# RWKV-6 attention woven into an MLP mixer: the loads of r and k as pieces of their own, the halves of y around the next unit's state products and gram, new sequences

## Chip, core and metric

The kernel runs on one core of one Trainium2 chip. The metric is the device time of one execution in microseconds (us). Five engines run side by side: PE (TensorE, matmul), DVE (VectorE), ACT (ScalarE), POOL (GpSimd) and SP (SyncE, which issues nearly all transfers). Each works through its own instructions in program order and waits for the others by semaphores.

## The reference

Attention in four batches, eight heads of 48, 768 steps; its output is laid out as (batch, 768, 384) and goes through a mixer over tokens (768 to 256 to 768) and one over channels (384 to 1536 to 384).

```python
for t in range(S):
    cur = einsum('bhd,bhe->bhde', u[None] * k[t], v[t])
    y[t] = einsum('bhd,bhde->bhe', r[t], state + cur)
    state = w[t][..., None] * state + einsum('bhd,bhe->bhde', k[t], v[t])
x = y.transpose(0, 2, 1, 3).reshape(B, S, H * D)

h = maximum(x.transpose(0, 2, 1) @ w_tok1, 0) @ w_tok2
u = x + h.transpose(0, 2, 1)
out = u + maximum(u @ w_ch1, 0) @ w_ch2
```

All of it is float32.

## The kernel before

**Units.** The 768 steps of a batch are cut into three units of 256 steps (two chunks of 128 rows); there are twelve, 0 to 11, and units 3b to 3b + 2 are batch b. For a unit DVE builds products of the decays w by two scans (`ends`, L435, and `begins`, L443), multiplies k by the one (`keys`, L440) and r by the other (`queries`, L446). PE transposes the keys (`tokens`, L345, into k_ps), ACT copies them out (`copied0`, `copied1`, L350), and PE forms k times v for the state (`carry`, L365, the state products, into kv_ps). ACT and DVE take turns at carrying the state over four steps (`by0` to `by3`, L501, and `up0` to `up3`, L514 and L516). `gram` (L315) is r times k within 64 steps, masked by DVE (`mask`, L488), which releases its two banks. `sums0` to `sums2` and `put` (L463 to L473) put in the diagonal.

**The two halves of y.** `before` (L380) multiplies r by the states that stood before each block, into two banks of y_ps; ACT reads one column of each (`seen`, L392), and `after` (L401) adds the part from within the blocks, with vt and at. ACT copies y to x in three pieces (`taken0` to `taken2`, L407); `taken0` releases the first bank, `taken1` and `taken2` the second. `tokens`, `carry`, `gram`, `before` and `after` are each made of many small products, 8 transposes or 64 matmuls of 64 by 48 or 64 elements.

**Dependencies between units.** `keys` of a unit needs the loads that the unit before it started; `by1` of a unit needs `before` of the unit before, `mask` needs its `after`, and the load of v is issued behind `after` and `carry`.

**The mixer** of a batch: `hidden` (L662) forms the first token sums from the six chunks of x, two chunks for each unit; `back` (L693, L702) the second; `turn` (L708) transposes, with forms by ACT (L710) and DVE (L711), joined at L634. The channel part takes two half batches of 384 columns, each in two halves of six sums. An up sum is nine products of 128x384: three at L739, three at L741 with a weight tile from the ring, three at L746. ACT (L721, L724), DVE (L728) and POOL (L732) make the three forms of it (`high`, `scaled`, `z`). `down` (L757 to L759) multiplies these by the second weights, three products for each sum and each 128 columns; DVE adds the result to x (L765), SP stores it (L767). A ring of ten tiles holds the third forms of the weights; each use of a tile is followed by the load of another (L625, `load_third`), which waits on SP until that use is done. Batch 0's mixer is made of other lines (back L903, turn L914, up L934 and L938, down L949, the sum L953).

**PSUM.** kv_ps has banks of its own. All else takes turns in six banks (`bank`): y two, gram two, the transposed keys two, each wide sum one.

**Order.** Batch 0's attention runs in a prologue in an order written out by hand (to about 48 us). After it the mixer of batch bt is woven with the attention of batch bt + 1 by a string `WEAVES[bt]`: `interleaved` takes the next piece of the stream that each digit names. Stream 0 is the mixer (from batch 1 on it has a second for joins, from batch 2 on more for its token weights' forms); the units have one stream each, as the function `attention_pieces` lists them; in batches 0 and 1 a last stream forms weights. The string sets the order on PE, DVE, ACT and SP at once; every engine works its own instructions in that order. Each unit's stream begins with `loads`, which is `load_rk(i + 1)`: four transfers of 192 KB on SP (L168), the halves of k first. Since a unit's pieces stand in one stream, their order among themselves is fixed by the function, `loads` ahead of all others.

How PE's pieces of a unit (number behind the name) stand among the mixer's pieces (the plain numbers count those), from the three strings; braces hold what follows without a piece of the mixer between:

```
batch 0: 19 {tokens3 own3} 7 {carry3 gram3} 11 {before3} 2 {after3} 13 {tokens4} 6 {carry4 gram4} 12 {before4} 4
         {tokens5} 3 {carry5 after4 gram5} 7 {before5} 1 {after5} 1
batch 1: 12 {tokens6} 3 {carry6 gram6} 19 {before6} 11 {tokens7} 9 {after6 carry7 gram7} 18 {before7} 11
         {tokens8} 5 {carry8 gram8 after7} 13 {before8} 2 {after8} 13
batch 2: 12 {tokens9} 7 {carry9} 7 {gram9} 21 {before9} 5 {tokens10} 8 {carry10 gram10 after9} 17 {before10} 9
         {tokens11} 2 {after10 carry11 gram11} 19 {before11} 2 {after11} 13
```

(`own` is a gram of a batch's first unit with u times k.)

Of the kernel before, what the change touches and what calls it, by code (L numbers as in the profile page):

```python
# [47 lines left out]
LEAST, MOST = 2.0 ** -40, 2.0 ** 40  # L48
MID = 3 * G // 4 * SEG1
WEAVES = [  # L50
    "44140440440000440401041114001004140004404040411441110104414014401041041014144110144140104404110140444000414141004140414"
    "442044444104440214401040404000424420404012404240024022400042242242420242244422044040204442200422044422000202443003334030"
    "43040303443332342344343300343243434334034343243304404300344342403333",
    "050000022220000505250502225052502205522502012100010252000000220200002000200002200200020002000220300000300200330033003030"
    "033000000000030000023330330302000033303033003330000000101103000003300040020400000000204300000040044000444000404443304444"
    "4044040000000440404000400000044003040004040000300444000000000000",
    "204240000022033204220000433322344240400000044440010001100404440000000000044000004040040000400044004000400400404055550000"
    "050505000500000000055000450055450005055055540550500045005050500001101050505606000000000006000400000660606666065606060000"
    "066005066050606660000606000605600000606000600006060660006000000000000000",
    "200202020202023002300320320003300000000011100000000000000000000000000000000000000000000000000000000000000000000000000000"  # L60
    "00001101000000000000000000000000000000000000000000000000000000000000000000000000000000000",
]


# [1 line left out]
def rwkv6_then_mixer(  # L66
# [950 lines left out]
    def interleaved(order, *streams):  # L1017

        left_of = [iter(stream) for stream in streams]
        out = [next(left_of[int(n)])[1] for n in order]  # L1020
        assert not any(True for stream in left_of for _ in stream)
        return out
# [116 lines left out]

    units = {i: unit(i) for i in range(UB, NU)}  # L1140
    attention = {bt: [attention_pieces(i) for i in range(bt * UB, (bt + 1) * UB)] for bt in range(1, B)}

    for bt in range(B):
        if bt == 0:
            early_forms, late_forms = weights_in_turn()
            pieces = interleaved(WEAVES[0], first_mixing(), *attention[1], early_forms)
        elif bt < B - 1:
            pieces = interleaved(WEAVES[bt], *exact_mixing(bt), *attention[bt + 1], *([late_forms] if bt == 1 else []))
        else:
            pieces = interleaved(WEAVES[bt], *exact_mixing(bt))  # L1150
# [134 lines left out]
```

## Time and profile before

| | us |
|---|---|
| median of three runs | 481.99 |
| the three runs | 480.54, 481.99, 482.96 |
| the profiled execution | 482.32 |
| its span in the profile | 480.5 |

The profile is of one execution. A row of the timeline has its start in us, the time from the start of its first instruction to the end of its last, the engine, the line of the kernel, the operation, what it writes and reads, and how many instructions stand in it; in brackets, the time that the engine stood idle before it and what released it. The ends of matmuls are modelled, so durations of neighbours overlap; their starts are what to count with. A row of waits has the engine and the line that waited, the releaser, the total, the number and the longest. A row of the windows has the stretch, then the busy time and the instructions of PE, PE's weight loads, DVE, ACT and POOL, then the granted clock of PE, the share of the transfer engines and their GB/s. A row of a tile has the line, the operation, the count, the shortest, median and longest duration in ns, and its first and last start.

### The profile page before, as it was taken

The page shows a single profiled execution, that of the slowest core. Times are in us where ns is not written, and L with a number is a line of the kernel's source. Part 1 is how long each engine was busy: PE and PEld are TensorE (multiplying, and loading weights), DVE is VectorE, ACT ScalarE, POOL GpSimd, SP SyncE. Part 2 cuts the span into 40 slices and gives each one's busy share as a digit, 9 for nine tenths or more (in the row PEclk, how much of TensorE's full clock was granted, in tenths as well). Part 3 has the DMA queues.
Part 4 walks back from the last instruction along what each step waited for, and adds up shares of the span by engine and source line. Part 5 has one row for each costly group of instructions (what it writes and reads, how often), then busy time and mean ns, then how long its engine had stood idle before and what let it go on. Part 6 is the DMA issues. An engine that isn't in the chain of part 4 may idle for free.

```text
span 480.5 us, 12671 instructions
## 1 busy us (share of the span) xinstructions
PE 464.9 (97%) x5298; PEld 408.3 (85%) x5298; DVE 336.4 (70%) x478; ACT 254.0 (53%) x588; POOL 59.2 (12%) x58
## 2 busy tenths in 40 slices
PE   2999999999999999999999999999999999999995
PEld 2786688866697668999999969999999979999995
DVE  7999899798788778757856298767856365235331
ACT  6689866763779666354546245365536244034040
POOL 1000000000000001230504002140413003032030
PEclk9999999999999999999999999999999999999999
DMA  8956937760684656764847553395605532436221
GB/s 302 330 166 205 280 130 232 260 218 33 179 245 138 194 170 213 218 217 155 229 132 246 205 163 128 116 267 184 191 26 175 193 103 83 121 94 206 87 86 56
DMA packets 49408, 83.77 MB, mean 174 GB/s; under 512 B 4864, under 2 KB 40576, under 8 KB 49344
## 3 DMA queue, kind: packets, MB, share of 16 engines
q1 hardware_dynamic: 49056, 82.80, 54.5%
q8 instruction: 43, 0.70, 0.6%
q14 instruction: 21, 0.17, 0.1%
q10 hardware_dynamic: 288, 0.10, 0.1%
HBM read 71.87 MB, written 11.01 MB: 172 GB/s over the span
## 4 chain that ended last, share of the span: by engine, by line
PE 95%; ACT 2%; DMA 1%; issue 0%; SPq 0%; DVE 0%; DVEq 0%; ACTq 0%
PE h_ps L949 10%; PE ends_ps L739 8%; PE ends_ps L746 8%; PE ends_ps L741 8%; PE o_ps L757 8%; PE o_ps L759 8%; PE o_ps L758 8%; PE z_ps L938 7%; PE h_ps L662 5%; PE gram L315 4%; PE z_ps L934 3%; PE h_ps L693 3%; PE y_ps L380 3%; PE y_ps L401 3%; PE kv_ps L365 2%; PE k_ps L345 2%
## 5 line engine op out<-in xcount | busy, mean ns | idle before, releaser
L732 POOL TENSOR_TENSOR z_high<-z_high 128x384 fp32r<-128x384 f32 x48 | 58.0, 1211 | 404.8 <-DMA ring<-third 188.2
L765 DVE SCALAR_TENSOR_TENSOR x<-o_ps,x 128x384 f32<-128x384 f32 x35 | 19.1, 556 | 54.9 <-PE o_ps L759 54.9
L721 ACT ACTIVATE z_high<-ends_ps 128x384 fp32r<-128x384 f32 x48 | 23.5, 489 | 58.3 <-PE ends_ps L746 58.2
L739 PE MATMUL ends_ps<-x_forms,forms 128*128 128x384 f32 x216 | 50.4, 341 | 0.0
L746 PE MATMUL ends_ps<-z_more,forms 128*128 128x384 f32 x216 | 50.2, 340 | 0.0
L741 PE MATMUL ends_ps<-x_forms,ring 128*128 128x384 f32 x216 | 49.3, 337 | 0.0
L949 PE MATMUL h_ps<-wch,z 128*128 128x384 f32 x144 | 48.6, 490 | 0.0
L728 DVE SCALAR_TENSOR_TENSOR z_high<-ends_ps,z_high 128x384 fp32r<-128x384 f32 x48 | 26.6, 553 | 31.0 <-ACT z_high L721 30.6
L757 PE MATMUL o_ps<-forms,z_high 128*128 128x384 f32 x140 | 47.9, 342 | 0.0
L759 PE MATMUL o_ps<-forms,z_high 128*128 128x384 f32 x140 | 47.1, 337 | 0.0
L758 PE MATMUL o_ps<-ring,z_high 128*128 128x384 f32 x140 | 47.1, 337 | 0.0
L501 ACT ACTIVATE before<-state,to_end 112x48 f32<-112x48 f32 x132 | 33.2, 323 | 18.2 <-DVE state L516 15.9
L949 PEld LDWEIGHTS h_ps<-wch,z 128*128 128x128 f32 x144 | 26.6, 190 | 16.8
L746 PEld LDWEIGHTS ends_ps<-z_more,forms 128*128 128x128 f32 x216 | 38.9, 188 | 0.3 <-DVE z_more L634 0.2
L739 PEld LDWEIGHTS ends_ps<-x_forms,forms 128*128 128x128 f32 x216 | 38.2, 188 | 0.7
L741 PEld LDWEIGHTS ends_ps<-x_forms,ring 128*128 128x128 f32 x216 | 38.5, 188 | 0.0
L938 PE MATMUL z_ps<-xT,wch 128*128 128x256 f32 x144 | 31.8, 380 | 0.0
L938 PEld LDWEIGHTS z_ps<-xT,wch 128*128 128x128 f32 x144 | 27.1, 190 | 3.8
L724 ACT ACTIVATE z_high<-z_high 128x384 fp32r<-128x384 f32 x48 | 25.2, 526 | 3.3
L757 PEld LDWEIGHTS o_ps<-forms,z_high 128*128 128x128 f32 x140 | 26.3, 188 | 0.2
L758 PEld LDWEIGHTS o_ps<-ring,z_high 128*128 128x128 f32 x140 | 26.3, 188 | 0.0
L759 PEld LDWEIGHTS o_ps<-forms,z_high 128*128 128x128 f32 x140 | 26.3, 188 | 0.0
(198 smaller groups left out, 929.6 us busy)
## 6 DMA issues: line engine op xcount, KB each, us to landing
ring<-third SPq DMA_DIRECT2D x144, 192.0 KB, 3.3
raw<-in_w_ch_dram SPq DMA_DIRECT2D x16, 512.0 KB, 4.9
rk<-in_rk_dram SPq DMA_DIRECT2D x36, 192.0 KB, 5.1
near<-in_near_dram SPq DMA_DIRECT2D x8, 768.0 KB, 4.9
w<-in_w_dram SPq DMA_DIRECT2D x10, 520.5 KB, 3.8
vt<-in_v_dram SPq DMA_DIRECT2D x12, 384.0 KB, 4.2
out_dram<-x SPq DMA_DIRECT2D x17, 192.0 KB, 2.5
third<-forms SPq DMA_DIRECT2D x12, 192.0 KB, 3.5
```

The source lines that it names most:

```text
L501: act.mul(t[:ROWS, a], state[bt, g][:ROWS, a], by_last(c, j)[:, a:a + 1])
L724: act.mul(z_form(jt, 2), z_form(jt, 0).bitcast(f32), 1.0 / BASE)
L728: dve.scalar_tensor_tensor(z_form(jt, 1), a, 0.0, z_form(jt, 0).bitcast(f32), op0=ALU.max, op1=ALU.subtract)
L732: pool.tensor_add(z_form(jt, 2), z_form(jt, 2).bitcast(f32), z_form(jt, 1).bitcast(f32))
L739: pe.matmul(a, up[m], xf[0][:, m], start=m == 0, stop=False)
L741: pe.matmul(a, low[:, m], xf[1][:, m], start=False, stop=False)
L746: pe.matmul(banks["a", jt], joint, xf[2][:, m], start=False, stop=m == 2)
L757: pe.matmul(a, z[0], up, start=first, stop=False, skip_group_check=True)
L758: pe.matmul(a, z[1], held[bt, s, half, 1, jt], start=False, stop=False, skip_group_check=True)
L759: pe.matmul(a, z[2], joint, start=False, stop=last, skip_group_check=True)
L938: pe.matmul(ps, now["wch1"][:, m, ts(jt, 128)], xT[:, m, ts(s, SEG)], start=(m == 0), stop=(m == DM // 128 - 1))
L949: pe.matmul(ps, zs[s][:, jt, ts(n, 128)], now["wch2"][:, jt, :], start=(jt == 0), stop=(jt == NJ - 1))
```

## The change

The first piece (`loads`) of each of the three units of a batch is taken out of the unit's stream, and the three form a stream of their own, so that a string can place them anywhere in their order. The streams behind move by one digit. Four new strings are put in. The prologue, the pieces and what each of them waits for are as before.

```diff
@@ -48,17 +48,17 @@
 WEAVES = [
-    "44140440440000440401041114001004140004404040411441110104414014401041041014144110144140144104404110140444000414141004140414"
...
+    "555500055500550050050010510155550505511055500505000551050550511511045515055511010505550105155150051151555151505510515505"
...
 ]
@@ -1139,6 +1139,8 @@
     units = {i: unit(i) for i in range(UB, NU)}
     attention = {bt: [attention_pieces(i) for i in range(bt * UB, (bt + 1) * UB)] for bt in range(1, B)}
+    for of in attention.values():
+        of.append([pieces.pop(0) for pieces in of])

     for bt in range(B):
         if bt == 0:
```

PE's order by the new strings, written as above:

```
batch 0: 25 {tokens3} 1 {own3} 8 {carry3 gram3} 22 {tokens4} 1 {before3 carry4 gram4 after3} 15 {tokens5} 5
         {before4 carry5 gram5 after4} 7 {before5} 1 {after5} 1
batch 1: 12 {tokens6} 6 {carry6 gram6} 39 {tokens7} 11 {carry7 before6 gram7 after6} 30 {tokens8} 5
         {before7 carry8 gram8 after7} 13 {before8 after8}
batch 2: 12 {tokens9} 12 {carry9 gram9} 30 {tokens10} 8 {before9 carry10 gram10 after9} 28 {tokens11} 6
         {carry11 before10 gram11 after10} 20 {before11} 3 {after11} 3
```

In batch 1 `taken2` of unit 7 stands behind unit 8's three copies. In batch 2 the loads for unit 11 stand behind the first six products of the third up sum of the second half batch; between these and the transposes of unit 11's keys PE has that sum's last three products, three more up sums and two groups of three products of `down`. `taken1` and `taken2` of unit 9 stand behind `taken1` of unit 10. Batch 3 has the mixer alone; its string changes the place of some forms and joins at its beginning.

More of the change, by code (lines that the diff above doesn't have):

```diff
@@ L50 @@
 WEAVES = [
[L51 to L60, printed above, removed]
@@ L61 @@
-    "00001101000000000000000000000000000000000000000000000000000000000000000000000000000000000",
+    "555500055500550050050010510155550505511055500505000551050550511511045515055511010505550105155150051151555151505510515505"
+    "015511515555000155550555502000050000002052525002212250215225155251252124552202500502222252055000025050005102333033350020"
+    "3331555035502235323535323550335400353533530305330355503305322353355",
+    "026000020266002066000062002662202000122526210010660260000002000000000002002000002002000022002220203300000000000000000000"
@@ new lines @@
+    "000003000003000300303322300000000303213221130030203000003300000500300300300003000003303300424000200000000000000003444344"
+    "4040000000400030344530004404444004000400004044344400304004444443",
+    "000000404240427220230220330223324034040400004040000111440400040000004004004400000040000000440004000044455000500000000000"
+    "055400054000500000000005005545450405050055555550004055050010001100550000600000070000000000060000600000666660005060606556"
+    "566606066666000066570060000000000000000000000000000564466006000660560660",
@@ L62 @@
+    "002000000022222230330202330002300000010001100000000000000000000000000000000000000000000000000000000000000000000000000000"
+    "00001010100000000000000000000000000000000000000000000000000000000000000000000000000000000",
 ]
```

## The prediction

> **What bounds the kernel now.** I read the page's totals and slices first, then the waits of the matmul engine, four windows by stage, and last the timeline around single units of attention.
>
> ```profile
> span 480.5 us, 12671 instructions
> PE 464.9 (97%) x5298; PEld 408.3 (85%) x5298; DVE 336.4 (70%) x478; ACT 254.0 (53%) x588; POOL 59.2 (12%) x58
> PE   2999999999999999999999999999999999999995
> PE 95%; ACT 2%; DMA 1%; issue 0%; SPq 0%; DVE 0%; DVEq 0%; ACTq 0%
> ```
> ```profile
> PE gram L315 <- ACT near L331: 8.5, 1, 8.5
> PE kv_ps L508 <- ACT before L501: 1.2, 2, 1.0
> PE h_ps L693 <- ACT z_high L686: 0.2, 1, 0.2
> ```
> ```profile
> 0.00:12.00 12.00, 3.54 (x72) 3.23 (x72) 8.48 (x13) 7.47 (x16) 1.26 (x10) 1.00 0.84 303
> 48.00:60.00 12.00, 12.00 (x47) 7.45 (x46) 10.33 (x15) 10.31 (x16) 0.00 (x0) 1.00 0.95 281
> 276.00:288.00 12.00, 11.75 (x52) 8.25 (x50) 11.47 (x15) 5.96 (x10) 0.00 (x0) 1.00 0.57 166
> 456.00:468.00 12.00, 12.00 (x71) 12.00 (x70) 5.02 (x9) 5.06 (x10) 4.05 (x4) 1.00 0.31 95
> ```
>
> PE is busy for 97% of the span and carries 95% of the chain that ended last. Its waits are one of 8.5 us and two of together 1.2 us, both in the prologue, which the change leaves alone, and one of 0.2 us behind it. The windows show what this means by stage: 3.54 of 12 us at the start, 12.00 of 12 from 48 us on, 11.75 where the one late wait falls, at a granted clock of 1.00. So the time after the prologue is the sum of what PE executes, in whatever order. A new order can change it in two ways only: by what it costs PE to go from one kind of product to another, and by making PE wait where it does not now.
>
> **The change, part by part.** The number of matmuls, copies and transfers is the same. What moves is their place.
>
> **Halves of y in runs.** A half of y is 64 small products. One that stands alone among the mixer's 128x384 products:
>
> ```profile
> 231.04 0.70 PE L746 MATMUL ends_ps<-z_more,forms 128*128 128x384 f32 x3
> 231.68 1.15 PE L380 MATMUL y_ps<-before,rk 48*64 48x48 f32 x64
> 232.75 0.80 PE L739 MATMUL ends_ps<-x_forms,forms 128*128 128x384 f32 x3
> 233.39 0.69 PE L741 MATMUL ends_ps<-x_forms,ring 128*128 128x384 f32 x3
> 233.91 0.70 PE L746 MATMUL ends_ps<-z_more,forms 128*128 128x384 f32 x3
> ```
>
> I count from start to start, since the ends are modelled. Three wide products take 0.52 (233.39 to 233.91), but 0.64 ahead of the half and 0.64 behind it; the half takes 1.07. Alone it costs 1.07 + 0.12 + 0.12 = 1.31 us. A half in a run with the state products and the gram:
>
> ```profile
> 214.56 0.69 PE L746 MATMUL ends_ps<-z_more,forms 128*128 128x384 f32 x3
> 215.18 1.15 PE L401 MATMUL y_ps<-vt,at 64*64 64x48 f32 x64
> 216.14 0.90 PE L365 MATMUL kv_ps<-vt,kT 64*48 64x48 f32 x64
> 216.86 1.13 PE L315 MATMUL gram<-rk 48*64 48x64 f32 x64
> 217.92 0.79 PE L739 MATMUL ends_ps<-x_forms,forms 128*128 128x384 f32 x3
> ```
>
> Followed by small products it takes 0.96 (215.18 to 216.14), and the run's two ends are paid by its neighbours anyhow. Joining a lone half saves 1.31 - 0.96 = 0.35. By the two sequences, seven halves that stand alone now come into such runs: both of unit 3 (with unit 4's state products and gram), the first of units 4, 6, 7, 9 and 10. 7 x 0.35 = **-2.45**; bounds 0 (if the gap is not one of switching) and -2.45.
>
> [...]
>
> **State products and gram of unit 9** stand apart now and together then: one entry and one exit fewer, but their neighbours are partly small transposes. Bounds 0 and -0.35, I take the middle, **-0.2**. Moving unit 3's own-gram one wide piece off the transposed keys I cost at nothing (bounds -0.1 and +0.1, the 0.12 of an edge), because the transposes leave no edge behind:
>
> ```profile
> 116.62 0.93 PE L345 MATMUL k_ps<-ident,rk 112*128 112x112 f32 x8
> 117.39 7.92 PE L949 MATMUL h_ps<-wch,z 128*128 128x384 f32 x24
> ```
>
> **The 0.25 us wait** of PE at 284.53 goes: ACT's form there is issued earlier against PE in the new sequence. Bounds 0 and -0.25, **-0.25**.
>
> ```profile
> 284.53 2.35 PE L693 MATMUL h_ps<-z_more,z_high 128*128 128x384 f32 x12 [0.25 <-ACT z_high L686]
> ```
>
> **Unit 8's halves** become neighbours at the end of batch 1's mixing. Between them ACT must read the first (`seen`), which now lies beside wide products:
>
> ```profile
> 163.14 1.15 PE L380 MATMUL y_ps<-before,rk 48*64 48x48 f32 x64
> 164.36 0.22 ACT L392 COPY seen<-y_ps 128x1 f32<-128x1 f32 x2 [1.13 <-PE y_ps L380]
> 164.60 0.47 ACT L407 COPY x<-y_ps 64x384 f32<-64x384 f32 x1
> 166.79 4.14 PE L662 MATMUL h_ps<-x,wtok 128*128 128x384 f32 x12
> 166.89 1.45 ACT L407 COPY x<-y_ps 128x384 f32<-128x384 f32 x3 [0.95 <-PE y_ps L401]
> ```
>
> The second half can start 164.58 - 163.14 = 1.44 after the first. The pair then costs 0.12 + 1.44 + 1.07 + 0.12 = 2.75, against 2 x 1.31 = 2.62 now: **+0.15** (0 if PE's queue hides part of it).
>
> **The first token sums of batch 2** stand right behind. Unit 7's last copy now follows three of unit 8 on ACT; four copies are done 0.10 + 1.45 + 0.47 = 2.0 us after the half ends. The sums of batch 1 took 4.14 for six chunks, 0.69 each, so the third chunk, which needs unit 7, is due at 1.4. **+0.6** (0 to 0.65).
>
> **Loads of r and k.** Each is four transfers on SP's in-order queue; the piece of unit i loads for unit i + 1, so that of unit 11 loads nothing. Seven of the eight others keep ten and more wide sums on PE between them and the transposes that need them, over 15 us. The one for unit 11 comes in batch 2 behind a ring load, which waits for PE's third up sum of that half. Until the transposes of unit 11's keys PE then has 0.52, three sums of nine products and two `down` groups: 0.52 + 3 x 1.57 + 2 x 0.52 = 6.3 us.
>
> ```profile
> SPq L625 <- PE ends_ps L741: 80.8, 57, 13.5
> L168 SPq DMA_DIRECT2D rk<-in_rk_dram x40: 310/420/1327, 1.7 to 313.7; - x40
> L440 DVE TENSOR_TENSOR rk<-rk,to_end x10: 1160/1212/1219, 17.9 to 343.6; 112x1024 f32<-112x1024 f32 x10
> DMA to landing us min/median/max: 3.0/5.2/9.3
> 312.34 1.81 SPq L168 DMA_DIRECT2D rk<-in_rk_dram  x4
> ```
>
> The k halves are issued first: the ring load and two issues at 0.42, a landing, and the keys' product of 1.21: 2.47 + 3.0 = 5.5 us, by the median 7.7, by the longest 11.8. PE would wait 0, 1.4 or 5.5 us. I take **+0.5**, nearer the shortest than the median, since the k halves are the first two of the four that the median counts. The wait holds `keys` on DVE; queued behind it are the `z` of the next up sums, `begins`, `queries` and `up3` of unit 10, so it is paid once, at the transposes or at the `down` products that need `z`. The quartet keeps SP from its ring loads for 1.8 us (312.34); the ring is ten tiles deep, at 0.52 us a tile at the quickest, which covers that; without it 1.8 us at each of the eight, 14 in all.
>
> [...] The trace's shortest landing is 3.0.
>
> `mask` of each next unit also waits for the half that now ends a run. Behind it on DVE are `sums2` and `put`; 7 and more wide pieces stand before the next half, so nothing is added.
>
> **Sum:** -2.45 - 0.2 - 0.25 + 0.15 + 0.6 + 0.5 = -1.65. Against the profiled execution's own 482.32 (its span of 480.5 and 1.8 around it) that is 480.7. It lies 0.33 over the median of the three runs, 481.99, so on the median the forecast is **480.3**. Its own range, with the landing and the joins as unknowns, is 479.0 to 481.8. What a measurement of this kernel can tell from no change is about 0.5%, 2.41 us: the forecast is inside it.
>
> **Rivals.**
> *No new wait.* Joins -2.45, unit 9 -0.35, the wait -0.25, unit 8's pair +0.15: -2.90, **479.1**. For it: the shortest landing. Against: the order of the copies on ACT. Chance 0.16.
>
> *The joins save nothing*, because the gap at an edge is refilled elsewhere: then only -0.25 + 0.15 + 0.6 + 0.5 = +1.0, **483.0**. For it: PE's sums are otherwise gapless, so the edge may be the modelled length of 64 short products. Against: 0.64 and 0.52 are differences of starts. Chance 0.12.
>
> *Unit 11's keys late (slower).* Place: the transposes of unit 11 in batch 2. If the k halves take the longest landing, 9.3, PE waits 5.5 in place of 0.5: -1.65 + 5.0 = +3.3, **485.3**. It decides from a landing of 3.8 (where the wait starts); the whole is no gain from 6.0, and slower than 0.5% from 8.4. For it: ring loads lie in the same queue ahead. Against: the median of 5.2. Chance 0.12.
>
> *Too few banks.* A run holds two y and two gram banks of six at once; in unit 11's, one bank of unit 9's y is still held as well. The next wide sums then wait for releases. With two banks a sum returns its bank after
>
> ```profile
> 231.78 0.49 ACT L721 ACTIVATE z_high<-ends_ps 128x384 fp32r<-128x384 f32 x1 [3.18 <-PE ends_ps L746]
> 232.37 0.56 DVE L728 SCALAR_TENSOR_TENSOR z_high<-ends_ps,z_high 128x384 fp32r<-128x384 f32 x1 [0.32 <-ACT z_high L721]
> 233.01 2.33 DVE L435 TENSOR_TENSOR_SCAN to_end<-w,starts 112x1041 f32<-112x1041 f32 x1
> ```
>
> 232.93 - 231.74 = 1.2 us, and sums come every 1.57, so 2 x 1.57 - 1.57 - 1.2 = 0.4 us are to spare; a scan of 2.33 in between costs 1.9. In two of the seven runs that is 3.8: -1.65 + 3.8, **484.1**. Against: the gram's banks are released before the next scan in the sequences. [...] No row here shows such a wait. Chance 0.08.
>
> That leaves 0.52 for the forecast.
>
> **How the numbers follow.** Faster by over 0.5% is below 479.6: three quarters of the first rival (0.12) and a quarter of the forecast (0.14): 0.26. Slower by over 0.5% is above 484.4: 0.08 of the late keys, 0.04 of the banks, 0.01 of the forecast: 0.13. The rest, 0.61, is no change that can be told. The range reaches 0.7 below the first rival, half of what the quickest of the three runs shown (480.54) lies below their median, and as much above the second (483.0): 478.4 to 483.6. Outside are most of the late keys and banks, some 0.16, and 0.04 below.
>
> **What would show it.** Right: lone halves gone for seven units' halves, with about 0.96 from start to start inside runs of four; PE's waits list with entries of 0.5 or less at the transposes of unit 11 (k_ps, released by the keys' product) and at the token sums of batch 2 (released by copies of y). Wrong: 1.07 and more inside the runs, a wait of PE over 1.5 us for unit 11's keys, or waits of PE for copies and `z` behind the runs. The whole would be wrong if PE's busy time after 48 us rose, since no instruction is added.

## The result and the profile after

The changed kernel takes 486.5 us (median of six runs, 485.99 to 488.13) against 481.74 for the kernel before (480.54 to 482.96, six runs): a ratio of 1.0108, interval 1.0081 to 1.0135. It is 1% slower, outside the range of the prediction. The profiled execution took 486.75, its span is 485.0.

The page of the changed kernel: span and busy times, PE and its granted clock in 40 slices, the row of a transfer queue that brings instructions, and the chain that ended last.

```profile
span 485.0 us, 12673 instructions
PE 462.0 (95%) x5298; PEld 407.0 (84%) x5298; DVE 340.0 (70%) x478; ACT 253.8 (52%) x588; POOL 59.7 (12%) x58
PE   3799999999999999998997999999999999999995
PEclk9889999999999999999998999999999999999998
q8 instruction: 43, 0.70, 0.6%
PE 86%; DMA 5%; ACT 3%; DVE 2%; issue 2%; POOL 1%; SPq 1%; DVEq 0%; ACTq 0%
```

PE executes as many matmuls as before (5298) and is busy for 462.0 us in place of 464.9. Nearly all of this difference lies in the prologue, though: the windows from the first `back` of batch 0 to the end, before and then after, have 425.08 and 424.98 us of PE, in 430.84 and 436.59 us.

```profile
49.66:480.50 430.84, 425.08 (x4303) 376.52 (x4301) 291.82 (x430) 216.86 (x491) 57.98 (x48) 1.00 0.53 165
48.41:485.00 436.59, 424.98 (x4303) 377.88 (x4301) 295.80 (x430) 216.75 (x491) 58.39 (x48) 0.99 0.53 162
```

So PE is busy for as long as before, a stretch at half its clock (below) included; what it has now is holes, in slices 19 and 22 (the dip of the clock in slices 2 and 3 lies in the prologue), and PE's share of the chain falls from 95 to 86%. The waits of PE (total, number, longest):

```profile
PE gram L315 <- ACT near L331: 8.4, 1, 8.4
PE y_ps L401 <- issue: 5.0, 2, 3.6
PE kv_ps L508 <- ACT before L501: 1.2, 2, 1.0
PE k_ps L345 <- PE kv_ps L508: 0.9, 1, 0.9
PE y_ps L401 <- ACT seen L389: 0.6, 1, 0.6
PE kv_ps L365 <- DVE state L516: 0.6, 1, 0.6
PE h_ps L662 <- ACT x L407: 0.4, 1, 0.4
PE y_ps L401 <- ACT seen L392: 0.3, 1, 0.3
PE k_ps L345 <- DVE rk L440: 0.2, 1, 0.2
```

The second row is new and large: two waits, 5.0 us together, in the second half of y, and "issue" means that PE waited for nothing that the profile shows. To place the loss, the spans are cut at rows that both kernels have: the first `back` of batch 0 (L903) and the first token sums of the other batches (L662). Before, then after:

```profile
49.66 1.66 PE L903 MATMUL kv_ps<-h,wtok 128*128 128x384 f32 x4
166.79 8.01 PE L662 MATMUL h_ps<-x,wtok 128*128 128x384 f32 x24
275.25 7.90 PE L662 MATMUL h_ps<-x,x_forms 128*128 128x384 f32 x24
382.89 7.90 PE L662 MATMUL h_ps<-x,x_forms 128*128 128x384 f32 x24
```
```profile
48.41 1.66 PE L903 MATMUL kv_ps<-h,wtok 128*128 128x384 f32 x4
164.60 8.01 PE L662 MATMUL h_ps<-x,wtok 128*128 128x384 f32 x24
279.66 1.56 PE L662 MATMUL h_ps<-x,x_forms 128*128 128x384 f32 x4
281.59 6.72 PE L662 MATMUL h_ps<-x,x_forms 128*128 128x384 f32 x20 [0.37 <-ACT x L407]
387.93 7.90 PE L662 MATMUL h_ps<-x,x_forms 128*128 128x384 f32 x24
```

Batch 0 takes 116.19 in place of 117.13, batch 1 115.06 in place of 108.46, batch 2 108.27 in place of 107.64. (The prologue, which the change leaves alone, was 1.25 us shorter in this execution.) So batch 0 gained 0.9, and batch 1 lost 6.6. This is batch 1's run around unit 8's gram, the timeline of PE in the changed kernel:

```profile
256.89 1.15 PE L380 MATMUL y_ps<-before,rk 48*64 48x48 f32 x64
257.86 0.83 PE L365 MATMUL kv_ps<-vt,kT 64*48 64x48 f32 x45
258.58 1.11 PE L315 MATMUL gram<-rk 48*64 48x64 f32 x61
259.49 0.35 PE L401 MATMUL y_ps<-vt,at 64*64 64x48 f32 x8
263.45 1.49 PE L401 MATMUL y_ps<-vt,at 64*64 64x48 f32 x55 [3.61 <-issue]
264.88 1.33 PE L739 MATMUL ends_ps<-x_forms,forms 128*128 128x384 f32 x3
266.00 1.16 PE L741 MATMUL ends_ps<-x_forms,ring 128*128 128x384 f32 x3
```

The half of y breaks off after a few of its 64 products, stands still for 3.61 us and goes on. Its data was probably there, since the first products of it had run. And what follows is slow: three wide products take 1.12 from start to start (264.88 to 266.00), not 0.52. The windows of the changed kernel (PE, weight loads, DVE, ACT, POOL, then the granted clock) say why, and they hold a second thing:

```profile
263.82:267.20 3.38, 3.38 (x54) 3.29 (x45) 0.00 (x0) 0.00 (x0) 0.00 (x0) 0.50 0.13 30
226.53:263.44 36.91, 33.30 (x381) 32.84 (x381) 26.32 (x38) 18.30 (x50) 10.01 (x8) 1.00 0.71 204
```

Just after the idle time PE was granted half its clock for 3.4 us. By an estimate from that length about 1.7 us of work were lost beside the 3.6. The second window reaches from the end of the other such wait (1.34 us, 226.54, in the run around unit 7's gram) to this one. It holds 381 matmuls and 381 weight loads; with the six semaphore instructions that the row does not count these are 768 records of PE, three times 256. The row of the instruction queue above has 43 packets with 0.70 MB, 16 KB each; 43 times 256 is 11008, room for the 10712 records that PE has in the trace. I read this as PE's program coming in packets of 256, and PE standing still where one packet ended and the next was not there. PE broke off behind 5825 records in the one place and behind 6593 in the other, 22 and 25 times 256 and then 193. The experiments test it.

### The profile page after: what moved, and what is told of

Same layout as the page of the kernel before. It is cut to its first block, busy times and chain, and to the rows that moved or that the text cites. A ratio compares the mean times of both kernels' runs of the same rounds, so it can differ in the third digit from the quotient of the medians.

```text
span 485.0 us, 12673 instructions
## 1 busy us (share of the span) xinstructions
PE 462.0 (95%) x5298; PEld 407.0 (84%) x5298; DVE 340.0 (70%) x478; ACT 253.8 (52%) x588; POOL 59.7 (12%) x58
## 4 chain that ended last, share of the span: by engine, by line
PE 86%; DMA 5%; ACT 3%; DVE 2%; issue 2%; POOL 1%; SPq 1%; DVEq 0%; ACTq 0%
PE h_ps L949 10%; PE o_ps L757 7%; PE o_ps L759 7%; PE o_ps L758 7%; PE ends_ps L739 7%; PE ends_ps L741 7%; PE ends_ps L746 7%; PE z_ps L938 6%; PE h_ps L662 5%; PE gram L315 3%; PE y_ps L401 3%; PE z_ps L934 3%; PE h_ps L693 3%; PE y_ps L380 2%; PE kv_ps L365 2%
## 5 line engine op out<-in xcount | busy, mean ns | idle before, releaser
L721 ACT ACTIVATE z_high<-ends_ps 128x384 fp32r<-128x384 f32 x48 | 23.5, 490 | 70.8 <-PE ends_ps L746 68.5
```

## The experiments

**Theory A:** PE's instructions are fetched a packet of 256 ahead; in a run of small products PE uses a packet up in some 1.9 us (two groups of 64, 0.96 us each), less than it takes to bring the next. The place between two packets is called a border below, and records are counted from the start of a run. In the changed kernel PE passed a border in unit 7's run at 223.05; a packet started at 224.02 and was in at 225.05, and PE went on at 226.54 from the next border, 3.49 us behind the first. Where two borders fall within such a run, PE waits. **Theory B:** runs of four groups are too long wherever they lie. **Theory C:** a half of y waits for data, in a way that the profile doesn't show. All batch lengths below are cut as above; batch 3 ends at the start of PE's last product.

**Borders moved, first try, and a control.** Small float32 products into columns of kv_ps that nothing reads:

```diff
+    def small_products(n):
+        for i in range(n):
+            q, j = ((0, 0), (1, 1), (0, 1), (1, 0))[i % 4]
+            pe.matmul(kv[q * P:q * P + D, j, 400:400 + D], ident[ts(j, T), ts(q, D)], ident[ts(j, T), ts(q, D)], ...)
...
+        if bt == 1: pieces.insert(25, lambda: small_products(70))
+        if bt == 2: pieces.insert(41, lambda: small_products(58))
```

> The changed kernel with 70 small products (140 instruction records on PE) added early in batch 1 and 58 (116 records) early in batch 2, into columns of kv_ps that nothing reads; the order of everything else stays. Theory A (PE runs out of instructions: its program comes in packets of 256 instructions, 43 packets of 16 KB in the profile, and a run of four small groups is through the next packet before that has come, where the packet's border lies between about a tenth and the half of the run): the borders in the runs of units 7 and 8 move from 178 and 116 records behind the run's start to 38 and to 232, those of batch 2 stay; the idle times of 1.6 and 3.8 us inside these runs and the 3.4 us at half clock (1.7 us) go. 486.5 - 1.6 - 3.8 - 1.7 + 1.3 + 1.1 for the added products = 481.8. Theory B (a run of four is too long whatever its place): nothing is saved, 486.5 + 2.4 = 488.9 with the two idle times as they were. Theory C (the second half of y waits for data of ACT, DVE or a transfer that the profile does not show): 488.9 too.

> The changed kernel with 128 small products (256 records, one whole packet) added early in batch 1, into columns that nothing reads. Theory A: every border lies where it lay relative to the runs, so the idle times inside the runs of units 7 and 8 stay, at 178 + 256 = 434 and 116 + 256 = 372 records behind the start; 486.5 + 2.1 = 488.6. Theories B and C: the same time. It is the control of the run with 70 and 58: the added work alone must not cure the stalls.

Measured 490.46 (ratio 1.0185, 1.0145 to 1.0226) and 492.32 (1.022, 1.0194 to 1.0246). The first expectation was wrong in its own count: a float32 product is four records (the 256 products of the long stretch below have 512 matmuls, and as many weight loads), so 70 of them moved the borders by 280 - 256 = 24 and not by 140, and no cure could be seen. But that shift is a test by itself. In the timeline of the first kernel the waits moved with the border, and in unit 8's run from the half of y into the gram:

```profile
228.48 0.78 PE L401 MATMUL y_ps<-vt,at 64*64 64x48 f32 x35 [1.10 <-issue]
264.62 0.27 PE L315 MATMUL gram<-rk 48*64 48x64 f32 x2 [2.79 <-issue]
```

Counted from the start of the run they lie at records 410 and 348 in place of 434 and 372, 24 earlier both. In the control, where 128 products are 512 records and so two whole packets, they stayed at 434 and 372. It took 3.7 us more than expected: its added products are a dense stretch of their own, and PE stood still in it for 1.91 us, again at a border. Theory C falls: the gram does not use what the half of y uses.

**Transfers behind the run.** Unit 9's loads of r and k (four transfers, which the new stream had placed inside unit 8's run) go behind it, in batch 1's string; then, in a kernel of its own, the load of w (piece 242) as well as they (259).

```diff
-    "4040000000400030344530004404444004000400004044344400304004444443",
+    "4040000000400030344300045404444004000400004044344400304004444443",
...
+        if bt == 1:
+            for at in (259, 242):
+                pieces.insert(264, pieces.pop(at))
```

> The changed kernel with one piece moved: the loads of r and k of unit 9 (four transfers of 192 KB) stand behind unit 8's run and the load of v on SP, no longer in the middle of the run. PE's order and its borders stay. Theory A: the packet that unit 8's run needs was on its way 3.1 us late, behind these transfers; it starts some 1 us after the border as the others do, the idle time of 3.8 falls to about 1.6 as in unit 7's run, and PE keeps its full clock or loses part of 1.7: 486.5 - 2.2 to 486.5 - 3.9 = 482.6 to 484.3. Theories B and C (unless it is this transfer that the half of y waits for, in which case the idle time goes wholly, 481.0): 486.5.

> As the run with unit 9's loads of r and k behind unit 8's run, and the load of w (520 KB) behind it too; no transfer but two ring loads of 192 KB is then issued ahead of the border in unit 8's run. With r and k alone moved the packet started 2.63 us behind the border in place of 3.12 and the idle time was 2.99 in place of 3.82, with w still 1 us ahead of the border. Theory A: the packet starts 0.9 to 1.1 us behind the border as in unit 7's run, the idle time falls to about 1.4, at 372 records, and batch 1 takes 112.2 - 1.5 = 110.7. The time: 486.5 - 4.3 = 482.2 (to 483.5, as a late w can be late for batch 2). If the transfers have nothing to do with it: 112.2 again.

Unit 8's run in the first kernel and in the second:

```profile
263.89 1.03 PE L401 MATMUL y_ps<-vt,at 64*64 64x48 f32 x55 [2.77 <-issue]
```
```profile
263.45 1.03 PE L401 MATMUL y_ps<-vt,at 64*64 64x48 f32 x55 [1.40 <-issue]
```

In the changed kernel the packet that unit 8's run lacked went out 3.12 us after PE had passed the border before it (260.87 against 257.74), and PE went on 1.6 us after it was in (261.83). With the loads of r and k away it started 2.63 late, with w away too 0.88, near the 0.97 of unit 7's run; the wait went 3.61, 2.77, 1.40. Batch 1 took 115.06, 112.23, 111.44. The length of the long wait goes with the transfers around it; with none but ring loads there it is that of unit 7's (1.34), and both kernels keep their full clock there. The time is lower for the second kernel, 483.98 (1.0056, 1.003 to 1.0081; 482.2 to 483.5 was expected), not for the first: 487.23 (1.0118, 1.0092 to 1.0144), though its profiled execution took 485.63. Why its three other runs took 487.1 to 488.1 is open. Half the clock for 3.4 us behind the wait, which the profiled execution did not have, would explain about 1.7 us; the mean granted clock of a run (0.984 to 0.991 in these, 0.997 in the profiled one) doesn't show it, as in the changed kernel the runs at 0.984 to 0.987 were the quicker ones, 486.0 to 486.8, and those at 0.991 and 0.995 took 488.1.

**The run cut.** Unit 7's second half behind the next up sum:

```diff
+        if bt == 1:
+            pieces.insert(263, pieces.pop(260))
```

> The changed kernel with the second half of unit 7's y behind the next up sum (nine wide products, 1.57 us) in place of inside unit 8's run, which then has three members. The border at 372 records lies in the gram, ahead of where the run is cut. Theory A: the idle time of 3 to 4 us stays, at 372 records, and the half standing alone costs 0.35: 486.9 (486.5 to 487.3). Theory B: a run of three does not stall, 486.5 - 3.8 - 1.7 + 0.35 = 481.4. Theory C: the wait, if it is one of that half, is covered by 1.57 us, 485 to 481.

483.81 (1.003, 1.0008 to 1.0051); batch 1 takes 112.45. The time is between the two theories, and the reason is a miscount: `carry` of a batch's last unit has 24 products and so 96 records, not 128, and the run of three ends at 354 and the border at 372 lies behind it. PE got 1.57 us of wide products on its way to the border, and waited for what was left:

```profile
262.53 0.68 PE L746 MATMUL ends_ps<-z_more,forms 128*128 128x384 f32 x3
264.64 1.15 PE L401 MATMUL y_ps<-vt,at 64*64 64x48 f32 x64 [1.43 <-ACT z_more L721]
```

The row names ACT, but its L721 had ended 0.54 us before PE went on (264.10), where PE starts less than 0.1 us behind ACT in the waits that ACT did end (0.05 at 281.59 in the changed kernel); what this half needs of ACT, `seen`, was done at 260.08. PE broke off again behind 6593 records, at the border, and went on 1.5 us after the packet was in. From border to border it took 5.15 us, 5.71 in the changed kernel. Against theory B: PE stood still behind a run of three too, and behind wide products.

**Borders moved, second try.**

```diff
+        if bt == 1: pieces.insert(25, lambda: small_products(35))
+        if bt == 2: pieces.insert(41, lambda: small_products(29))
```

> The changed kernel with 35 small products early in batch 1 and 29 early in batch 2, which write columns that nothing reads. Each float32 product is four records on PE (two weight loads, two matmuls), as the rows of the run with 70 and 58 show: its borders moved by 280 - 256 = 24 records and not by 140. Now the shift is 140 and then 116, together one packet. Theory A (PE runs out of instructions at a packet's border): the borders in the runs of units 7 and 8 go to 38 and 232 records behind the start, those of batch 2 stay; no idle time inside a run in batch 1. Batch 1 takes 115.06 - 1.56 - 3.82 - 1.7 (half clock) + 1.3 (the products) = 109.3 in place of 115.06 us, batch 2 108.3 + 1.1 = 109.4, all in all 486.5 - 4.7 = 481.8. Theory B (a run of four is too long wherever it lies) and theory C (a wait for data): 488.9.

488.3 (1.0114, 1.0079 to 1.015): not the cure; batch 1 took 113.90, not 109.3. In unit 7's run, with the border at 38, the wait is at the next one, 294, and 0.43 in place of 1.34. In unit 8's, the border went to 232 and the next to 488, which I had taken for harmless since the run ends at 482; it is not:

```profile
261.32 0.79 PE L739 MATMUL ends_ps<-x_forms,forms 128*128 128x384 f32 x3
264.55 1.33 PE L741 MATMUL ends_ps<-x_forms,ring 128*128 128x384 f32 x3 [2.44 <-issue]
```

Now the wide products behind the run wait. They could not wait for the run's data, nor for its length; what this stop shares with the others is the border, 256 records behind the one before (488 and 232). Two smaller stops at borders, 0.61 us in batch 0 and 0.44 in batch 2, are in this profile as well.

**The same harm done to the kernel before.** Its runs of three have only one border each. 25 products, early in batch 1, and nothing else:

```diff
+        if bt == 1: pieces.insert(25, lambda: small_products(25))
```

> The kernel before, its sequences as they were, with 25 small products (100 records) early in batch 1. Its runs of three have their borders at 203 and 128 records (batch 1) and 205 and 190 (batch 2), so that the next one lies behind the run's end; shifted they are 103, 28, 105 and 90, and 359, 361 and 346 records lie inside runs of 384, 384 and 354. Theory A: three idle times of PE of about 1.4 us, at those borders, in a kernel that had none: 481.8 + 0.9 + 4.2 = 486.9. Theory B (only runs of four): 482.7. Theory C: 482.7.

490.97 (1.0173, 1.0129 to 1.0218), 8.7 us for 25 small products. Three waits that the kernel before doesn't have, in the three runs named, at records 359, 361 and 346:

```profile
219.85 0.45 PE L315 MATMUL gram<-rk 48*64 48x64 f32 x13 [1.52 <-issue]
331.82 0.43 PE L401 MATMUL y_ps<-vt,at 64*64 64x48 f32 x12 [2.50 <-issue]
361.36 0.33 PE L315 MATMUL gram<-rk 48*64 48x64 f32 x4 [1.06 <-issue]
```

The fourth run (borders at 28 and 284) has none. The time is 4 us over the expectation: the middle wait was longer than 1.4, its packet started 2.3 us behind its border, with a load of w ahead of it, and the profile has two stretches of 3.4 us at half clock, behind the first and the second of these waits. This settles theory A against B: the kernel's old order is hurt by the place of its borders alone.

**The supply by itself.** 256 small products in one stretch in batch 3 of the kernel before; and the same in eight groups among wide products.

```diff
+        if bt == 3: pieces.insert(100, lambda: small_products(256))
```

> The kernel before with one stretch of 256 small products (1024 records, four packets) in batch 3, where the transfer engines are a third busy; they write columns that nothing reads. It measures the supply of instructions by itself. Theory A with one packet fetched ahead: in a steady stretch each packet costs what it takes from border to border where PE waited with little traffic, 3.3 to 3.5 us, so idle times of about 1.4 us at the borders behind the first or second, 256 records apart: 482.2 + 7.5 (512 matmuls by 0.94 for 64) + 0.2 + 2 to 4 times 1.4 = 492.7 to 495.5. [...]

> The same 256 small products in batch 3, in eight groups of 32 (128 records, half a packet) with six to some twenty wide products of the mixer between them; they write columns that nothing reads. Theory A: 128 records in 0.97 us and 18 of nine wide products in 1.57 us are 256 records in about 4.5 us, more than the 3.4 to 3.7 that a packet took in the single stretch: no idle time at a border. Batch 3 takes 91.75 + 7.5 + 8 x 0.24 (edges) = 101.2 in place of the stretch's 105.94. If the waits of the stretch belonged to the products and not to their density, 105.9 plus the edges.

```profile
421.29 2.28 PE L1146 MATMUL kv_ps<-ident 64*48 64x48 f32 x182
425.28 1.66 PE L1146 MATMUL kv_ps<-ident 64*48 64x48 f32 x128 [1.72 <-issue]
429.02 2.36 PE L1146 MATMUL kv_ps<-ident 64*48 64x48 f32 x128 [2.08 <-issue]
432.48 1.83 PE L1146 MATMUL kv_ps<-ident 64*48 64x48 f32 x74 [1.10 <-issue]
```

Each kernel has one run. The stretch comes in pieces of 128 matmuls (and as many weight loads, 256 records), one each 3.5 to 3.7 us (425.28, 429.02, 432.48). Its time is 495.89; batch 3 takes 105.94. Spread, the same products give 490.85 and 100.28, with no wait for issue among PE's waits. Spread, the 256 products cost 100.28 - 91.75 = 8.5 us; in one stretch 5.7 us more, of which 4.9 are the three waits. The rest is not accounted for; PE was granted half its clock for 6.8 us from behind the second wait on, which may be it.

**What is left without the waits.** Batch 1 as before, all else new; then batches 0 and 3 new and batches 1 and 2 as before. The second's edit is shown, without its strings; the first makes such streams for the units of batches 1 and 3:

```diff
-    for of in attention.values():
-        of.append([pieces.pop(0) for pieces in of])
...
+    attention[1].append([pieces.pop(0) for pieces in attention[1]])
```

> The changed kernel with batch 1's sequence of before (loads of batch 2's units at the head of their streams again); batches 0, 2 and 3 keep the new sequences, with runs of four in both. Theory A: no border falls badly in batches 0 and 2 (22 to 43 and 239 records behind the start), so only the gain of the joins is left: 481.7 - 0.9 for batch 0, and batch 2 between 0 and -0.6, as unit 7's copies no longer come late: 480.4 (479.9 to 481.0). Theory B: the four runs of batches 0 and 2 cost like those of batch 1, over 484. Theory C: about 481.

> The new sequences of batch 0 (three halves of y joined, loads as their own stream) and of batch 3, the old ones of batches 1 and 2. Its runs of four have a border 43 and 30 records behind their start, where PE was through without waiting in some of the profiles and waited 0.5 to 0.8 us at 299 records in others (batch 0 then took 117.1 in place of 116.2, against 117.1 before). Theory A: -0.9 to 0 for batch 0, -0.2 for batch 3, none of the long waits: 482.2 - 0.2 to 482.2 - 1.1 = 481.1 to 482.0. If runs of four cost by their length: over 484.

The first takes 482.37 (1.0016, 0.9997 to 1.0035), not the 480.4 expected, but the waits in runs are gone though batches 0 and 2 have their runs of four: theory B falls here too. What it lost is in batch 2, 109.67 in place of 107.64; among PE's waits are now

```profile
PE h_ps L693 <- DVE z_more L671: 0.6, 1, 0.6
PE kv_ps L365 <- DVE state L516: 0.6, 1, 0.6
PE k_ps L345 <- DVE rk L440: 0.4, 1, 0.4
```

The first of them (with one of 0.3 beside it) stands at the beginning of batch 2, where the new sequence meets the end of the old one; the other two are unit 11's and stand in the changed kernel as well.

The second kernel takes 480.12 against 481.35 beside it (12 and 17 runs; 0.9969, 0.9953 to 0.9985): it is faster than the kernel before by 0.3%, and the only one here that is. That is 1.2 us in place of the 0.2 to 1.1 expected. Batch 0 takes 116.19 and batch 3 91.59, as in the changed kernel (117.12 and 91.75 before).

## Why the prediction was wrong

**What bounds the kernel** was right as far as the trace of before went: PE back to back after the prologue. The step that failed stands in the same paragraph: "A new order can change it in two ways only: by what it costs PE to go from one kind of product to another, and by making PE wait where it does not now", where I looked for the waits among data, copies, banks and transfers. In their place the runs show two stops of 1.34 and 3.61 us in the runs of units 7 and 8, 768 records apart, which ended 1.5 and 1.6 us after a packet of the instruction queue had come in (225.05 and 261.83), and half the clock for 3.4 us behind the second. That PE was out of instructions there is my reading of this. PE's own program is a transfer too, and it was on the page (43 packets, 0.70 MB, on an instruction queue) but I did not read that row. From this came the bound that failed, "bounds 0 (if the gap is not one of switching) and -2.45" for the joins: joining halves into runs could save less or nothing but not cost, because I gave a longer run no way to cost anything. The sign named for the whole being wrong, a longer busy time of PE behind 48 us, did not come either (425.0 in place of 425.1): it looked for dearer work, and the loss is idle time. In the trace of before the runs of three had their borders at 128 to 205 records, one each, and the experiment with 25 products shows how near to the edge that was.

By batch the forecast of -1.65 is -1.05, -0.55 and -0.05; the profiled execution has -0.9, +6.6 and +0.6.

**The joins** themselves: -0.35 for each, three in batch 0 are -1.05; batch 0 measured -0.94, and -0.93 in the best kernel. Right, as long as the borders spare them: in three other profiles with the new order of batch 0 PE stopped at record 299 for 0.3 to 0.6 us, and batch 0 took 116.8 to 117.1, so that little or nothing of the gain was left.

**Batch 1**: joins -0.7 and unit 8's pair +0.15 make -0.55; measured +6.6. The two waits in runs (1.34 + 3.61), the half clock (some 1.7) and a wait of 0.3 for `seen` are 6.95; less the joins (0.7) and the two edges that the pair saves (0.24) that is 6.0, 0.6 short of what was measured; this rest is open. That the half clock costs 1.7 is worked out from its length; with the loads behind the run the half clock was gone and batch 1 took 2.83 less, of which the shorter waits explain about 1, and 1.7 would explain most of the rest.

**Unit 8's pair and the first token sums of batch 2**: `seen` let PE wait 0.3, and the third chunk 0.55 (281.59 - 279.66 - 4 x 0.345), against 0.6. Right, and small.

**Unit 11's keys**: +0.5 forecast; 0.2 for the keys and 0.6 for the state behind `up3`, which the prediction names in the queue behind them. The mechanism was right, though paid at two places and not once; the slower rival did not come. The wait of 0.25 at L693 went, as forecast. Of batch 2's +0.6 some 0.4 stay unexplained.

**Too few banks**: no wait of PE for a bank of a wide sum is in the list. **The joins save nothing**: refuted by batch 0. **Loads of r and k**: not only hidden or late; with them inside unit 8's run PE's packet started 3.12 us behind the border, with them behind it 2.63, which no case had.

## What to carry to other kernels

Before small products are joined, count the instructions. Here a dense stretch had some 1.9 us of work in 256 records, and where PE stood still the time from one packet's border to the next was 3.5 us in unit 7's run (223.05 to 226.54), 3.7 and 3.5 in the long stretch, and 5.7 in unit 8's run, under transfers. The sign of it was a stop in the middle of a group whose data was there, with no releaser; the number of records between two such stops (256 in the long stretch, 768 in the changed kernel) led to the packet. The order that was measured to be good depended on where those borders fell: 25 small products far ahead cost 8.7 us, against some 0.9 that was expected for their own work.

## What was not expected of the hardware

In the profiles of all of the runs above, every wait of PE that is put down to issue, from 20 us on, lies behind a number of records that is 193 more than a multiple of 256 (5825 and 6593 in the changed kernel); the kernel before, the best one and the one with the products spread have none. In the changed kernel it went on 1.49 and 1.62 us after the packet of 16 KB had come in (226.54 against 225.05, 263.45 against 261.83), which itself took 1.03 and 0.97 us. The packet started 0.97 us after the border before it in unit 7's run, and 0.88 in unit 8's with the transfers behind it; under the load of w it started 2.3 (shifted kernel before) and 2.63 us after (loads of r and k behind the run), under w, r and k 3.12. Borders in the first tenth of a run (22 to 43 records) cost nothing in the changed kernel and up to 0.6 us at the next border in other profiles: in the changed kernel the packet had started 0.82, 2.02 and 1.40 us before PE's first record behind the border (119.80, 146.26 and 326.30 against 120.62, 148.28 and 327.70). Why it was earlier there was not shown.

Behind the prologue the granted clock fell to 0.50 for 3.4 us after waits of 3.6 (changed kernel), 2.8 (the first try and its control), 2.5 (shifted kernel before) and 2.4 us (the second try), in the shifted kernel before after 1.5 as well, and for 6.8 us behind the second wait of the long stretch (2.1), but not after 2.8 with the loads behind the run, the first one of the long stretch (1.7) or 1.3 in the changed kernel. So the length of the wait alone does not tell these cases apart; no run moved a wait by itself, and what does was not shown. In the trace of the changed kernel the stretches of one granted clock between the first change and the last are 6.83, 235.52, 3.41 and 215.04 us long, of which those of 6.83 and 3.41 at 0.50.
